# Issuing four early loads from two queues, and loading the branch's integer one step earlier, in a fused windowed-attention and gated-conv kernel

## The chip, the cores and the metric

The kernel runs on one core of one Trainium2 chip. The metric is the device time of one execution in microseconds (us), as the median of several runs. Before the change it is 231.44 us (three runs, 230.78 to 232.59).

The core's engines named below are TensorE (PE), VectorE (DVE), ScalarE (ACT), GpSimd (POOL) and SyncE (SP). SP computes nothing here: it issues DMA transfers. ACT can issue them as well.

## The reference

Two stages over q, k, v of shape (8 batches, 8 heads, 576 positions, 64), in f32:

```python
scores = q @ k.transpose(0, 1, 3, 2) / sqrt(64)
scores = where(abs(pos_i - pos_j) <= 32, scores, -1e9)      # sliding window
attn   = exp(scores - max); attn = attn / (sum(attn) + 1e-9)
x      = (attn @ v).transpose(0, 2, 1, 3).reshape(8, 576, 512)

h    = maximum(x @ w_in, 0)                                  # 512 -> 1024
conv = sum over k of conv_w[k] * h shifted by k - 1          # 3 taps along the sequence
out  = (h * sigmoid(conv)) @ w_out                           # 1024 -> 512
```

The output has the shape (8, 576, 512), f32.

## The kernel before

The work is cut into named operations. An operation is a small piece: a load, a cast, a group of matmuls, a copy out of PSUM. `build` lists them with their dependencies, and the string `PLAN` gives the order in which they are written into the program, with the engine of each copy (`/A` is ACT, `/D` is DVE) and the PSUM banks (`@01`). Each operation is pinned behind what stands before it on its engine (`do`, which calls `keep_in_program_order`), so on each engine the order of PLAN is the order of execution. A few helper instructions are not pinned: the load of the convolution's weights `cw24` (line 399), GpSimd's masks, and `values_load` (line 774).

The operations of the beginning are these:

- `LQK0.yz` loads half z of the positions of k (y = 1) or q (y = 0) of batch 0 into a staging buffer `st` (line 449). It is issued as two transfers, one for each half of the heads (e = 0, 1), each 128 rows of 2,304 bytes, 288 KB. Six staging buffers are used in a ring; a later load into a buffer waits for the cast that reads it.
- `CQK0.yz` casts that buffer to bf16 (line 382 on DVE). It needs both halves.
- `TR0.yz` transposes it on PE (line 393), and `EV0.yz0` and `EV0.yz1` copy the result out of PSUM (line 380 on ACT, line 382 on DVE).
- `MK` builds the four masks and small identity matrices on DVE (lines 421 to 428). The block `start()` (lines 397 to 416) is written ahead of the first word of PLAN that isn't a load: memsets on DVE, a warming activation on ACT (line 398, which brings the load of ACT's function table with it), the issue of `cw24` on ACT, and GpSimd's identity and masks.
- `SC` are the score matmuls, `EX` the exponentials on ACT, `MA` the mask products on DVE, `AV` the products with v, and `F512` filler matmuls on zeros.

In PLAN before, three loads stand ahead of `MK`, and the fourth, LQK0.00, behind it. All eight transfers are issued by SP (`self.dq` is `nc.sync`). The casts follow in the order CQK0.11, CQK0.01, CQK0.10, CQK0.00, all on DVE.

From about 36 us to the end PE works through three streams mixed by PLAN: attention of later batches, the hidden layer (`PH`, relu `RE` on ACT), and the convolution and gate (`CO`, `TA` on ACT, `GA` on DVE) with the output product (`YY`, copy `YC`, store `YS`).

At the end stands a branch. The attention skips the subtraction of the maximum; `OK`, `OM` and `OF` test whether all sums were in range and leave an integer `bad`. `values_load` (line 774) loads it into a register on every engine, and `tc.If(bad > 0)` (line 775) goes to `redo`, a slow version of the whole kernel, if it isn't zero. With the inputs here it is zero: every engine branches past the code of `redo` to the closing barrier (line 802). In the program before, `values_load` is written behind everything else. The last words of PLAN are the output product in the parts YY11.1, YY11.0, YY11.2b and YY11.2a, whose copies are YC11.1 on DVE and YC11.0, YC11.2b and YC11.2a on ACT, each with a store of its own on SP (line 741).

Of the kernel before, what the change touches and what calls it, by code (L numbers as in the profile page):

```python
# [14 lines left out]
B, H, S, D, DM, DF = 8, 8, 576, 64, 512, 1024  # L15
KC, MB, RP, PAD = DM // 128, DF // 128, S // 64, 32
# [56 lines left out]
def build(k, ud=UD):  # L73
# [136 lines left out]

    add("MK", {"DVE": 2.4}, lambda e: k.consts(), w=["mk"])
    load_qk(0, (0,))
    load_qk(0, (1,))
    p = Slot()
    add("CW", {"PE": 0.3}, lambda e: k.conv_w(p), r=[("qkT", 0, y, z, 0) for y in range(2) for z in range(2)], w=["cw"],
# [5 lines left out]
    for u, tls in units():  # L221
        while done_b <= min(B - 1, (2 * u + tls[-1]) // 9):
            for parts in ((0,), (1,)) if done_b < HB else ((0, 1),):
                load_qk(done_b, parts)
            load_v(done_b)
            if done_b == 1:
                weights_out()
            done_b += 1
        attend(u, tls)
        while done_c < NCH and (u > 3 * done_c + 3 - (done_c % 3 == 2) or u == NU - 1) and tls[-1] == 1:  # L230
            ffn(done_c)
            done_c += 1
# [8 lines left out]


PLAN = """
LQK0.11 LQK0.01 LQK0.10 MK LQK0.00 CQK0.11/D LV0.1 TR0.11@01 CQK0.01/D EV0.111/A TR0.01@23 LQK1.00 EV0.110/A
EV0.011/D LQK1.10 CQK0.10/D EV0.010/D TR0.10@30 LV0.4 SC4a@21 CQK0.00/D LV0.2 SC3@45 EX4a.1 EV0.101/A EV0.100/D
LV0.0 TR0.00@16 EX4a.0 LWI3 EV0.001/A MA4a EV0.000/A EX3.1 SC1@16 LWI1 CQK1.00/D SC0@32 EX1.1 SC2@50 CV0.1/D EX0.1
TR1.00@67 LV0.3 EX2.1 CW@2 EV1.001/D EX0.0 EX2.0 CQK1.10/D LWI2 EV1.000/A LWI0 DG EX1.0 F512@0 F512@0 TR1.10@57
# [71 lines left out]
GA10.02 RE11.4 PH11.3@2 RE11.7 TA10.10 CO11.0@7345 RE11.3 GA10.10 PH11.5@6 RO11.1 TA11.00 PH11.1@0 RE11.5 TA11.01  # L319
RO11.3 OM@1 YY10.0@2 RO11.2/D RE11.1 TA11.02 OF GA11.00 TA11.03 GA11.02 CO11.1@7061 YC10.0/D YY10.1@4 GA11.01 TA11.11  # L320
TA11.12 GA11.11 TA11.10 GA11.12 TA11.13 GA11.10 YY10.2@0 YC10.1/A GA11.03 GA11.13 YY11.1@1 YC10.2/D YS10 YY11.0@0
YC11.1/D YS11.1 YY11.2b@1 YC11.0/A YY11.2a@5 YS11.0 YC11.2b/A YS11.2b YC11.2a/A YS11.2a
"""


class Kernel:
# [117 lines left out]
    def load_qk(self, b, y, z, s):  # L444
        st = self.st[s].rearrange("p (e x) -> p e x", e=2)
        if b < HB:
            for e in range(2):
                src = self.qk[y][b, 4 * e:4 * e + 4, 288 * z:, :]
                self.do(self.dq.dma_start(st[:, e], bass.AP(src.tensor, src.offset, [[RP * D, 32], [S * D, 4], [1, RP * D]])))
        else:  # L450
            src = self.qk[y][b, 2 * z:, :, :]
            self.do(self.dq.dma_start(st, bass.AP(src.tensor, src.offset, [[RP * D, 128], [4 * S * D, 2], [1, RP * D]])))
# [291 lines left out]
@with_exitstack  # L744
def kernel(
    ctx: ExitStack,
    tc: tile.TileContext,
    q: bass.AP,
    k: bass.AP,
    v: bass.AP,  # L750
    moe_w_in: bass.AP,
    moe_conv_w: bass.AP,
    moe_w_out: bass.AP,
    out: bass.AP,
):
    kn = Kernel(ctx, tc, q, k, v, moe_w_in, moe_conv_w, moe_w_out, out)
    ops = {op.name: op for op in build(kn).ops}
    names = {"A": "ACT", "D": "DVE", "P": "POOL", "S": "SP"}
    started = False
    for word in PLAN.split():  # L760
        word, _, where = word.partition("@")
        name, _, eng = word.partition("/")
        if not started and not name.startswith("L"):
            kn.start()
            started = True
        if name.startswith("F"):
            kn.fill(int(name[1:]), int(where))
            continue
        op = ops.pop(name)
        for slot, at in zip(op.alloc, where):  # L770
            slot.at = int(at)
        op.emit(names[eng] if eng else next(iter(op.cost)))
    assert not ops
    bad = kn.nc.values_load(kn.bad[0:1, 0:1], min_val=0, max_val=1)
    with tc.If(bad > 0, preferred_fallthrough_block=False):
        kn.redo()

# [29 lines left out]
```

## Time and profile before

| | |
|---|---|
| median of the runs | 231.44 us (230.78 to 232.59) |
| the profiled execution | 233.62 us |
| its span, first to last instruction | 231.9 us, 8,874 instructions |
| granted TensorE clock, mean | 0.991 |
| busy: PE, DVE, ACT | 208.9 us (90%), 190.4 us (82%), 180.5 us (78%) |
| moved by DMA | 49.45 MB, 213 GB/s on average |

The profile is one execution. The span counts from the first to the last instruction on the core; the time of an execution has a little around it. L449 is line 449 of the kernel. A name such as `st<-in_q_dram` says what was written from what. "SPq" and "ACTq" are the issuing queues of those engines, "PEld" the weight loads of TensorE. In a timeline a row gives the start in us, the length in us, the engine, the line and the operation; a bracket at the end gives the idle time ahead of it and what ended that. A chain of waits is followed back from the last instruction, at each step to what released it.

### The profile page before, as it was taken

How to read it: one execution, taken by the hardware profiler on the slowest of the kernel's cores; microseconds unless marked ns; L12 is line 12 of the kernel's file. 1: busy time of each engine (PE TensorE's matmuls, PEld its weight loads, DVE VectorE, ACT ScalarE, POOL GpSimd, SP SyncE). 2: the span in 40 equal slices, each digit the busy share in tenths (PEclk: the TensorE clock that was granted, in tenths of full speed). 3: DMA queues.
4: the chain of work that ended last, by engine and by line, in shares of the span. 5: the costliest groups of instructions: out<-in, count | busy, mean ns of one | idle time of the engine just before them, and what ended most of it. 6: DMA issues, size and time to landing. Idle time of an engine off the chain costs nothing.

```text
span 231.9 us, 8874 instructions
## 1 busy us (share of the span) xinstructions
PE 208.9 (90%) x3741; PEld 122.4 (53%) x3741; DVE 190.4 (82%) x459; ACT 180.5 (78%) x393; POOL 1.2 (1%) x8
## 2 busy tenths in 40 slices
PE   0479789999999999999999999999999879999990
PEld 0354467776455655555655555554545445545450
DVE  7668799999899999999988998889998686655820
ACT  2296688878999999789899989999679577559520
POOL 2000000000000000000000000000000000000000
PEclk9999999999999999999999999999999979999999
DMA  5999599698999994988995984998986926524161
GB/s 154 355 280 309 125 266 217 185 256 219 273 261 328 270 352 131 260 248 251 368 176 114 302 267 90 159 300 197 359 107 206 284 53 105 151 60 160 50 227 56
DMA packets 67187, 49.45 MB, mean 213 GB/s; under 512 B 48044, under 2 KB 53444, under 8 KB 67140
## 3 DMA queue, kind: packets, MB, share of 16 engines
q1 hardware_dynamic: 67104, 48.80, 79.6%
q8 instruction: 31, 0.51, 1.0%
q14 instruction: 16, 0.13, 0.2%
q10 hardware_dynamic: 36, 0.01, 0.0%
HBM read 32.52 MB, written 9.44 MB: 181 GB/s over the span
## 4 chain that ended last, share of the span: by engine, by line
PE 54%; DVE 21%; ACT 8%; DMA 7%; issue 4%; SPq 3%; DVEq 0%; ACTq 0%
PE ps L390 50%; DVE xn L634 5%; PE ps L393 4%; DMA st<-in_q_dram 4%; DVE gT L721 4%; DMA vst<-in_v_dram 3%; DVE vo L382 2%; ACT ps L714 2%; DVE attn L614 2%; ACT attn L543 2%; DVE qkb L382 2%; DVE rec L633 2%; ACT hh L681 2%; SPq L460 2%; DVE ve L382 1%
## 5 line engine op out<-in xcount | busy, mean ns | idle before, releaser
L390 PE MATMUL ps<-xT,w_in_sb 128*128 128x385 bf16 (+3 forms) x448 | 73.1, 308 | 1.0 <-DVE w_in_sb L382 0.3
L390 PE MATMUL ps<-w_out_sb,gT 128*128 128x512 bf16 (+1 forms) x296 | 67.4, 374 | 0.2
L681 ACT ACTIVATE hh<-ps 128x385 bf16<-128x385 f32 (+3 forms) x112 | 47.9, 474 | 10.4 <-PE ps L390 10.2
L721 DVE SCALAR_TENSOR_TENSOR gT<-ps,hh 128x384 bf16<-128x384 f32 x96 | 48.6, 549 | 8.3 <-ACT ps L714 7.2
L390 PEld LDWEIGHTS <-w_in_sb 128*128 128x128 bf16 x448 | 39.8, 99 | 24.6 <-issue 4.3
L714 ACT ACTIVATE ps<-ps 128x384 f32<-128x384 f32 x96 | 42.0, 495 | 6.8 <-PE ps L390 6.1
L543 ACT ACTIVATE attn<-ps 128x512 bf16<-128x512 f32 (+1 forms) x76 | 40.5, 612 | 7.0 <-PE ps L390 3.5
L390 PEld LDWEIGHTS <-gT 128*128 128x128 bf16 x296 | 27.2, 98 | 29.1 <-issue 1.3
L634 DVE TENSOR_TENSOR xn<-ps,rec 128x256 bf16<-128x256 f32 (+1 forms) x76 | 32.2, 424 | 2.6
L380 ACT COPY qkT<-ps 128x576 bf16<-128x576 bf16 x42 | 26.4, 669 | 7.1 <-PE ps L393 7.0
L614 DVE TENSOR_TENSOR attn<-attn,masks 128x1024 bf16<-128x1024 bf16 (+1 forms) x38 | 24.5, 658 | 2.6 <-ACT attn L543 2.4
L393 PE MATMUL ps<-ident,qkb 64*128 64x64 bf16 x576 | 14.5, 199 | 9.8 <-DVE qkb L382 9.1
L380 ACT COPY y<-ps 128x512 f32<-128x512 f32 (+1 forms) x27 | 16.3, 608 | 8.5 <-PE ps L390 8.5
L390 PE MATMUL ps<-hh,diag 32*32 32x384 bf16 x1152 | 20.5, 327 | 0.0
L393 PEld LDWEIGHTS <-qkb 64*128 64x128 bf16 x576 | 11.5, 100 | 15.9 <-DVE qkb L382 11.1
L390 PEld LDWEIGHTS <-attn 128*64 128x64 bf16 x576 | 13.1, 113 | 11.0 <-issue 5.1
L382 DVE COPY qkT<-ps 128x576 bf16<-128x576 bf16 x22 | 16.2, 750 | 2.8 <-PE ps L393 2.6
L382 DVE CAST qkb<-st 128x1152 bf16<-128x1152 f32 x22 | 16.6, 753 | 2.3 <-DMA st<-in_q_dram 2.1
L390 PE MATMUL ps<-ve,attn 128*64 128x65 bf16 x320 | 16.1, 200 | 1.4 <-DVE xn L634 1.0
L390 PEld LDWEIGHTS <-diag 32*32 32x32 bf16 x1152 | 11.9, 88 | 8.0 <-issue 4.4
L633 DVE RECIPROCAL rec<-ps 128x4 f32<-128x4 f32 (+1 forms) x76 | 13.2, 174 | 3.0 <-PE ps L390 2.6
L390 PE MATMUL ps<-vo,attn 128*64 128x65 bf16 x256 | 13.4, 199 | 2.4 <-DVE vo L382 2.1
(57 smaller groups left out, 137.0 us busy)
## 6 DMA issues: line engine op xcount, KB each, us to landing
out_dram<-y SPq DMA_DIRECT2D x11, 768.0 KB, 5.5
st<-in_k_dram SPq DMA_DIRECT2D x12, 576.0 KB, 7.1
st<-in_q_dram SPq DMA_DIRECT2D x12, 576.0 KB, 5.4
vst<-in_v_dram SPq DMA_DIRECT2D x24, 256.0 KB, 5.8
vst<-in_v_dram SPq DMA_DIRECT2D x16, 192.0 KB, 5.5
hh<-hh SPq DMA_DIRECT2D x16, 144.8 KB, 2.9
st<-in_k_dram SPq DMA_DIRECT2D x8, 288.0 KB, 4.8
st<-in_q_dram SPq DMA_DIRECT2D x8, 288.0 KB, 4.5
```

Of the source, the lines that this page charges most:

```text
L380: self.do(nc.scalar.copy(out=out, in_=in_))
L382: self.do(nc.vector.tensor_copy(out=out, in_=in_))
L390: self.do(self.nc.tensor.matmul(*a, **kw))
L393: self.do(self.nc.tensor.transpose(out=out, in_=in_, identity=ident))
L460: self.do(self.dq.dma_start(self.vst[s0 - lo:s1 - lo, c], self.v_[b, :, s0:s1, :].rearrange("h p d -> p h d")))
L543: self.do(self.nc.scalar.activation(at[:, lo:hi], self.ps(ps)[:, lo:hi], AF.Exp, bias=0.0, scale=self.scale))
L614: self.do(self.nc.vector.tensor_tensor(out=at, in0=at, in1=m, op=ALU.mult))
L633: self.do(self.nc.vector.reciprocal(rec, po[:, :, 64]))
L634: self.do(self.nc.vector.tensor_tensor(out=self.xn[x][lo:hi, 4 * g:4 * g + 4, :], in0=po[:, :, 0:64], in1=rec[:, :, None].broadcast_to([hi ...
L681: self.do(self.nc.scalar.activation(o, i_, AF.Relu, bias=0.0, scale=0.5))
L714: self.do(self.nc.scalar.activation(z, z, AF.Tanh, bias=0.0, scale=1.0))
L721: self.do(self.nc.vector.scalar_tensor_tensor(out=o, in0=z, scalar=1.0, in1=self.taps(kind, 0, 128, 6 + 2 * j + g if j else g, 1), op0=ALU ...
```

## The change

Three edits.

In PLAN the fourth load moves ahead of `MK`, and so ahead of the block `start()`. In `load_qk` the second half of the heads (e = 1) of each batch 0 load is issued by ACT, the first half still by SP. That holds for the main path alone; `redo` keeps its queue. And the `values_load` of `bad` becomes a word of PLAN, `VL`, which stands behind YY11.2a, the last matmuls, and ahead of the store of YY11.0 and of the copies and stores of YY11.2b and YY11.2a.

```diff
 PLAN = """
-LQK0.11 LQK0.01 LQK0.10 MK LQK0.00 CQK0.11/D LV0.1 TR0.11@01 ...
+LQK0.11 LQK0.01 LQK0.10 LQK0.00 MK CQK0.11/D LV0.1 TR0.11@01 ...
...
-YC11.1/D YS11.1 YY11.2b@1 YC11.0/A YY11.2a@5 YS11.0 YC11.2b/A YS11.2b YC11.2a/A YS11.2a
+YC11.1/D YS11.1 YY11.2b@1 YC11.0/A YY11.2a@5 VL YS11.0 YC11.2b/A YS11.2b YC11.2a/A YS11.2a
 """
...
         if b < HB:
             for e in range(2):
                 src = self.qk[y][b, 4 * e:4 * e + 4, 288 * z:, :]
-                self.do(self.dq.dma_start(st[:, e], bass.AP(...)))
+                dq = self.nc.scalar if b == 0 and e and not self.general else self.dq
+                self.do(dq.dma_start(st[:, e], bass.AP(...)))
...
+        if name == "VL":
+            bad = kn.nc.values_load(kn.bad[0:1, 0:1], min_val=0, max_val=1)
+            continue
         op = ops.pop(name)
...
     assert not ops
-    bad = kn.nc.values_load(kn.bad[0:1, 0:1], min_val=0, max_val=1)
     with tc.If(bad > 0, preferred_fallthrough_block=False):
         kn.redo()
```

More of the change, by code (lines that the diff above doesn't have):

```diff
@@ L243 @@
 PLAN = """
-LQK0.11 LQK0.01 LQK0.10 MK LQK0.00 CQK0.11/D LV0.1 TR0.11@01 CQK0.01/D EV0.111/A TR0.01@23 LQK1.00 EV0.110/A
+LQK0.11 LQK0.01 LQK0.10 LQK0.00 MK CQK0.11/D LV0.1 TR0.11@01 CQK0.01/D EV0.111/A TR0.01@23 LQK1.00 EV0.110/A
 EV0.011/D LQK1.10 CQK0.10/D EV0.010/D TR0.10@30 LV0.4 SC4a@21 CQK0.00/D LV0.2 SC3@45 EX4a.1 EV0.101/A EV0.100/D
@@ L448, in load_qk @@
                 src = self.qk[y][b, 4 * e:4 * e + 4, 288 * z:, :]
-                self.do(self.dq.dma_start(st[:, e], bass.AP(src.tensor, src.offset, [[RP * D, 32], [S * D, 4], [1, RP * D]])))
+                dq = self.nc.scalar if b == 0 and e and not self.general else self.dq
+                self.do(dq.dma_start(st[:, e], bass.AP(src.tensor, src.offset, [[RP * D, 32], [S * D, 4], [1, RP * D]])))
         else:
```

## The prediction

> **What bounds the kernel now.** I read the page first, then the chain of waits in order of time, then the timeline of the first 12 us and of the last 12 us, where the two edits lie.
>
> ```profile
> span 231.9 us, 8874 instructions
> ...
> PEclk9999999999999999999999999999999979999999
> ...
> PE 54%; DVE 21%; ACT 8%; DMA 7%; issue 4%; SPq 3%; DVEq 0%; ACTq 0%
> ```
>
> The chain that ended last runs over PE for 54% of the span and over VectorE for 21%: in the long middle the engines are full and neither edit touches them. Over transfers it runs for only 7%. The profiled execution took 233.62 us, 1.72 more than its span; the median of the runs is 231.44. One slice (185 to 191 us) had a granted clock of 0.7, and both edits lie outside it, so I take a saving found in the span off the median as it is.
>
> The front, from the chain of waits (start, length, what):
>
> ```profile
> 2.85 4.51 DMA st<-in_q_dram
> ...
> 7.46 0.77 DVE qkb L382
> ...
> 8.98 0.24 DVE qkT L382
> 9.21 0.44 issue
> 9.65 0.76 DVE qkb L382
> ...
> 18.12 6.03 PE ps L390 x31
> ...
> 54.65 0.61 DVE w_out_sb L382
> ...
> 55.27 5.28 DMA st<-in_q_dram
> ```
>
> The first transfer on it is the second half of the second load (LQK0.01, q), issued at 2.85 and landed at 2.85 + 4.51 = 7.36. Behind that stand the cast at 7.46, the transposes, the copy at 8.98, the next cast at 9.65, and so on. The timeline of the same stretch:
>
> ```profile
> 0.81 1.35 SPq L449 DMA_DIRECT2D st<-in_k_dram  x2
> 0.81 0.60 ACTq L399 DMA_DIRECT2D cw<-in_moe_conv_w_dram  x1
> ...
> 1.45 1.28 ACT L398 ACT_TABLE_LOAD   x1 [1.45 <-PEq L791]
> ...
> 2.20 1.25 SPq L449 DMA_DIRECT2D st<-in_q_dram  x2
> ...
> 4.85 0.70 DVE L428 COPY id<-ident 32x32 bf16<-32x32 bf16 x4
> 5.58 0.76 DVE L382 CAST qkb<-st 128x1152 bf16<-128x1152 f32 x1
> ...
> 7.10 1.18 ACT L380 COPY qkT<-ps 128x576 bf16<-128x576 bf16 x2 [4.16 <-PE ps L393]
> 7.46 0.76 DVE L382 CAST qkb<-st 128x1152 bf16<-128x1152 f32 x1 [1.11 <-DMA st<-in_q_dram]
> ...
> 10.46 0.66 PE L393 MATMUL ps<-ident,qkb 64*128 64x64 bf16 x18 [1.52 <-DVE qkb L382]
> ...
> 11.98 1.89 SPq L460 DMA_DIRECT2D vst<-in_v_dram  x1
> ```
>
> The first cast (CQK0.11, 5.58) waits for no transfer: VectorE is busy with the constants until 4.85 + 0.70 = 5.55. The second waits 1.11 us for the transfer. So a faster front is worth at most 1.11 us, and whatever makes the first load land earlier is worth nothing.
>
> **The change, part by part: the loads.** Eight issues leave SP, four of them go to ACT. Two issues take 1.25 to 1.35 us on SP, so about 0.6 each. Now the half issued third at 2.20 and the half issued fourth at 2.85 are both issued second on their queue, at 0.81 + 0.65 = 1.45: 0.75 and 1.4 us earlier. How much of that reaches the landing depends on how busy the transfer engines are. The table by stage gives, in its last three columns, granted clock, DMA share and GB/s:
>
> ```profile
> 2.00:3.00 1.00, 0.00 (x0) 0.00 (x0) 0.78 (x8) 0.93 (x2) 0.32 (x2) 1.00 0.64 106
> 3.00:4.00 1.00, 0.00 (x0) 0.00 (x0) 1.00 (x9) 0.00 (x0) 0.16 (x1) 1.00 1.00 387
> 4.00:5.00 1.00, 0.00 (x0) 0.00 (x0) 0.92 (x6) 0.00 (x0) 0.00 (x0) 1.00 0.87 219
> 5.00:6.00 1.00, 0.00 (x0) 0.00 (x0) 0.93 (x5) 0.00 (x0) 0.00 (x0) 1.00 0.84 263
> 6.00:7.00 1.00, 0.60 (x18) 0.50 (x18) 0.34 (x1) 0.00 (x0) 0.00 (x0) 1.00 1.04 399
> ```
>
> From 3 to 4 and from 6 to 7 they run full, at 387 and 399 GB/s. Between them is a hole, 219 and 263, just where q is first read: it loses (390 - 219 + 390 - 263) / 390 = 0.76 us. The start, 2 to 3 us, loses (390 - 106) / 390 = 0.73 more. A second queue can fill part of both, because two streams are then outstanding instead of one, but it can't pass 390 to 400. The first two loads are 4 x 288 KB = 1,180 thousand bytes. By the rows, 106 + 387 + 219 + 263 = 975 were through at 6.0 and all 1,180 at 6.5; the last engine landed at 7.36, 0.85 later. With the hole filled, the 1,074 that are left at 3.0 take 2.75 us, to 5.75; with the same lag the landing is 6.6, and the cast, 0.1 behind it, starts 0.75 us earlier. With the start filled too, VectorE is the limit (5.58 + 0.76 = 6.34) and the gain is the whole 1.11; with neither it is 0. I take 0.6, four fifths of the hole, since the first q packets of both halves now wait side by side. A loss on the front is the third rival.
>
> [...] No stage of this trace has two large streams at once. [...]
>
> What is late next is the third load: the cast at 9.65 follows the copy at 8.98 directly on VectorE, and its data has to be there at 9.65 - 0.6 = 9.05. It is 590 thousand bytes behind the second, 1.5 us at 390 GB/s, so 8.1 to 8.65: not late. From there the chain is engine work that starts when the step before it ends; the 6.03 us from 18.12 on are PE work in a fixed order, and the later transfer on the chain (55.27) begins where VectorE's cast of 54.65 ends. So the 0.6 stays to the end. SP runs past its issues sooner; the next load into a used buffer waits for the second cast, which moves with it.
>
> On ACT the four issues stand ahead of the table load and of the issue of cw: 0.81 + 4 x 0.65 + 0.60 + 1.28 + 0.20 (the warming activation) = 5.5, and its first copy is due at 7.10. That copy hangs on the first cast, which doesn't move, so 1.6 us of cover hide the move; without the cover ACT would be late by what goes over. Placing LQK0.00 ahead of MK and of the start-up block changes nothing on SP, where the four loads already stand back to back; on VectorE the constants keep their place.
>
> **The word VL.** ACT's last copies, from the timeline:
>
> ```profile
> 224.79 0.37 ACT L380 COPY y<-ps 128x256 f32<-128x256 f32 x1 [0.29 <-PE ps L390]
> 225.66 0.37 ACT L380 COPY y<-ps 128x256 f32<-128x256 f32 x1 [0.50 <-PE ps L390]
> ```
>
> The rows of lines 774 (load) and 775 (branch) (count, ns min/median/max, first and last start), and the last store with its time to landing:
>
> ```profile
> L774 PEldq TENSOR_LOAD <-bad x1: 767/767/767, 223.3 to 223.3; - x1
> L774 ACTq TENSOR_LOAD <-bad x1: 693/693/693, 225.7 to 225.7; - x1
> ...
> L775 PEldq COMPARE_BRANCH  x2: 95/2094/4093, 224.2 to 225.8; - x2
> L775 ACTq COMPARE_BRANCH  x2: 38/44/49, 226.4 to 226.6; - x2
> ...
> out_dram<-y SPq DMA_DIRECT2D x1, 128.0 KB, 3.6
> ```
>
> On PE the load already stands behind the last matmul's issue (223.3), so PE's order doesn't change: its second branch starts at 225.8, takes 4.09 us and ends at 229.9. The last store, issued when the copy of 225.66 ends (226.04) and landed 3.6 later, ends at 229.6. These two set the barrier that opens at 230.3 (row below), and VL moves neither. On ACT the load moves from behind the last copy to ahead of the last two: 0.69 us on an engine that is idle 0.29 and 0.50 before them. The copy of part 2b (224.79) and its store may be late by up to 0.69 - 0.29 = 0.40; the last copy isn't (224.79 + 0.40 + 0.37 = 225.56, due 225.66). ACT's second branch comes up to 0.5 earlier, at 226.1. By itself worth 0 for the barrier.
>
> **Four instructions more on ACT.** Behind the barrier (line 802, window from 230.25 on) one row stands out; below it are the code queues of the page:
>
> ```profile
> L802 ACTq EVENT_SEMAPHORE  x2: 17/17/17, 230.3 to 231.8; - x2
> ...
> L802 POOLq DRAIN  x2: 34/64/93, 230.3 to 230.7; - x2
> L802 SPq DRAIN  x1: 7/7/7, 230.4 to 230.4; - x1
> ...
> L802 PEldq DRAIN  x1: 8/8/8, 230.5 to 230.5; - x1
> ...
> L802 ACTq DRAIN  x1: 135/135/135, 231.5 to 231.5; - x1
> ...
> q8 instruction: 31, 0.51, 1.0%
> q14 instruction: 16, 0.13, 0.2%
> ```
>
> SP and PE drain 0.1 to 0.2 us after 230.3, ACT only at 231.5, with nothing to wait for, and all engines end at 231.8. Code arrives by transfer, 16 pieces of 8 KB on q14 and 31 of 16 KB on q8. PE's 2 x 3,741 instructions in 31 pieces are about 240 each, so the smaller pieces hold about 120. I read ACT's late drain as the first instruction of a new piece, reached too soon after the branch. Four DMA issues on ACT push its end four places further, so that the branch lands inside the new piece and nothing is left to wait for. Then POOL's drain at 230.7 is the next, and the end is 231.6 - 230.7 = 0.9 us earlier. The ends: 0 (the delay has another cause) and 0.95; with the cause right but the border still among ACT's last instructions, the earlier branch alone could give 0.5. I take 0.9. [...]
>
> The sum: 0.6 + 0.9 = 1.5 us; 231.9 becomes 230.4 in the span, and 231.44 becomes 229.9.
>
> **The rivals.** First, the front gives nothing: the engines ran at share 1.00 and 1.04 on both sides of the hole, and if the hole belongs to the first reading of q and not to a lone queue, two queues share the same wait. Against it: the shares of 0.64, 0.87 and 0.84 are room. It gives 231.44 - 0.9 = 230.5. [...]
>
> Second, the end gives nothing: ACT's late drain isn't a matter of place, or another engine, SP with four instructions fewer for one, meets a border in its last instructions. About 4 in 120 places do that, which speaks against the latter. 231.44 - 0.6 = 230.8.
>
> Third, slower: ACT's issues back up. The row at 11.98 shows an issue that took 1.89 us where the queue was full. ACT has until 7.10, so it decides from (7.10 - 0.81 - 2.08) / 4 = 1.05 us an issue. At 1.89 ACT is free at 0.81 + 7.56 + 2.08 = 10.45, its two copies end at 11.63, and the transposes of 10.46, which need the bank that the second copy frees, are 1.2 us late. Without the gain at the end that is 232.6, with it 231.7. Against it: at 1 to 3 us both queues are empty.
>
> Fourth, the scheduler undoes the moves (neither edit reaches the program's order): 231.4.
>
> **How the numbers follow.** Both gains 0.52 (229.9; own range 229.1 to 230.7, from a front of 0.2 to 1.1 and some 0.3 for the runs' median); the end alone 0.17 (230.5); the front alone 0.19 (230.8); slower through ACT 0.07 (231.7 to 232.6); nothing 0.05 (231.4). From 229.1 to 231.3 the range leaves out 2 in 10: the slower case, nothing, and the best of the first. A measurement of this kernel can tell about 1% from no change, 2.3 us: faster means under 229.1, which needs the full 1.11 and 0.95 and a lucky draw, 0.14; slower means over 233.8, 0.04; the rest is within 1%.
>
> **What would show it.** In the changed profile: L449 on both queues by 1.5 us; the second cast starting at 6.6 to 7.2 with less than 1.11 us of wait; the hole at 4 to 6 shallower; ACT's first copy still at 7.1; the chain from the copy at 8.98 on earlier by the same amount; PE's branch still 4.1 us; ACT's last drain within 0.3 us of the others. The prediction is wrong if the second load lands at 7.3 or later, if ACT's drain is still 1 us behind, if ACT's first copy is late, or if the front's gain is eaten by a new wait before 30 us.

## The result, and the profile after

The changed kernel took 228.02 us in the median of five runs (227.81 to 229.58), beside 231.44 us for the kernel before in the same measurement. The ratio is 0.986, 95% interval 0.983 to 0.990. The prediction was 229.9 us with a range of 229.1 to 231.3, so the time fell below the range. Measured twice more beside the kernel before, the same kernel gave ratios of 0.990 (0.985 to 0.995) and 0.989 (0.986 to 0.993). All its 23 runs together have a median of 228.79 us. Medians here are over all runs and ratios over the fast ones; the profiled execution of the kernel before, at 233.62 us, is one of the slow ones (over 1.5% above the fastest). The kernel before stood between 231.22 and 231.59 in the five groups of runs that hold a comparison. So the change is worth 2.7 us rather than the 1.5 us forecast, and about 0.8 us of the first reading was the scatter of five runs.

The profiled execution of the changed kernel took 229.58 us with a span of 227.9 us. Its head, and the line of the granted clock:

```profile
span 227.9 us, 8845 instructions
...
PEclk9999999999999999999999999999999999999998
...
PE 44%; DVE 24%; DMA 11%; ACT 9%; issue 5%; SPq 4%; DVEq 0%; ACTq 0%
```

The slice with a clock of 0.7 is not in every profile with the old loads: that of `vl_only` (below) shows none. So neither it nor the fall of TensorE's share of the chain of waits from 54 to 44% (47% in `vl_only`) is put down to the change. The timeline of its first 12 us, to be laid beside the one of before (in each row start, length, engine and line; a bracket names what the engine waited for):

```profile
0.81 0.72 SPq L450 DMA_DIRECT2D st<-in_k_dram  x1
0.81 0.65 ACTq L450 DMA_DIRECT2D st<-in_k_dram  x1
...
1.49 0.62 ACTq L450 DMA_DIRECT2D st<-in_q_dram  x1
1.59 0.79 SPq L450 DMA_DIRECT2D st<-in_q_dram  x1
...
2.79 0.62 ACTq L450 DMA_DIRECT2D st<-in_q_dram  x1
...
4.93 0.59 ACTq L399 DMA_DIRECT2D cw<-in_moe_conv_w_dram  x1
5.58 0.76 DVE L382 CAST qkb<-st 128x1152 bf16<-128x1152 f32 x1
...
7.10 1.18 ACT L380 COPY qkT<-ps 128x576 bf16<-128x576 bf16 x2 [2.16 <-PE ps L393]
8.31 0.76 DVE L382 CAST qkb<-st 128x1152 bf16<-128x1152 f32 x1 [1.97 <-DMA st<-in_q_dram]
```

The issues are where the prediction put them: both halves of the second load are under way by 1.59 us, ACT needs 0.62 to 0.65 us for one issue, and its first copy is still at 7.10. The table by stage shows the hole filled (the last three columns are granted clock, DMA share and GB/s; before it was 219 and 263 from 4 to 6 us):

```profile
4.00:5.00 1.00, 0.00 (x0) 0.00 (x0) 0.92 (x6) 0.94 (x2) 0.00 (x0) 1.00 1.05 403
5.00:6.00 1.00, 0.00 (x0) 0.00 (x0) 0.93 (x5) 0.00 (x0) 0.00 (x0) 1.00 1.06 360
```

And yet the second cast starts at 8.31, which is 0.85 us **later** than in the profile before (7.46), and it waits 1.97 us where before it waited 1.11. By this pair of profiles the front lost. How the kernel nevertheless became faster by more than forecast is the question of the experiments.

The end looks as forecast. The rows of the closing barrier (line 805 now; count, ns min/median/max, first and last start), and of the branch, line 778:

```profile
L805 ACTq EVENT_SEMAPHORE  x2: 17/17/17, 227.2 to 227.8; - x2
...
L805 POOLq DRAIN  x2: 34/64/93, 227.3 to 227.6; - x2
L805 ACTq DRAIN  x1: 8/8/8, 227.3 to 227.3; - x1
```

```profile
L778 PEldq COMPARE_BRANCH  x2: 95/1974/3853, 221.2 to 222.9; - x2
L778 ACTq COMPARE_BRANCH  x2: 38/46/53, 222.7 to 223.2; - x2
```

ACT's drain, 1.2 us behind the barrier before (231.5 against 230.3), now stands with it at 227.3, and it takes 8 ns where it took 135. The last wave of the barrier follows 0.6 us later (227.2 to 227.8), where it was 1.5 (230.3 to 231.8).

### The profile page after: what moved, and what is told of

Read it like the earlier page. It is cut to its first block, busy times and chain, and to the rows that moved or that the text cites. A ratio compares the mean times of both kernels' runs of the same rounds, so it can differ in the third digit from the quotient of the medians.

```text
span 227.9 us, 8845 instructions
## 1 busy us (share of the span) xinstructions
PE 203.4 (89%) x3711; PEld 121.1 (53%) x3741; DVE 190.1 (83%) x459; ACT 180.2 (79%) x393; POOL 1.2 (1%) x8
## 3 DMA queue, kind: packets, MB, share of 16 engines
HBM read 32.52 MB, written 9.44 MB: 184 GB/s over the span
## 4 chain that ended last, share of the span: by engine, by line
PE 44%; DVE 24%; DMA 11%; ACT 9%; issue 5%; SPq 4%; DVEq 0%; ACTq 0%
PE ps L390 41%; DMA vst<-in_v_dram 6%; DVE gT L722 5%; DVE xn L635 5%; PE ps L393 3%; DMA st<-in_q_dram 3%; ACT hh L682 3%; DVE attn L615 3%; ACT attn L544 2%; DVE vo L382 2%; DVE qkb L382 2%; ACT ps L715 2%; DVE rec L634 2%; DMA hh<-hh 2%; SPq L461 2%
## 5 line engine op out<-in xcount | busy, mean ns | idle before, releaser
L390 PE MATMUL ps<-xT,w_in_sb 128*128 128x385 bf16 (+3 forms) x448 | 72.3, 305 | 1.1 <-DVE w_in_sb L382 0.3
L390 PE MATMUL ps<-w_out_sb,gT 128*128 128x512 bf16 (+1 forms) x269 | 65.0, 373 | 1.8 <-issue 0.5
L390 PEld LDWEIGHTS <-attn 128*64 128x64 bf16 x576 | 12.6, 110 | 10.6 <-issue 5.2
L390 PE MATMUL ps<-ve,attn 128*64 128x65 bf16 x320 | 15.6, 197 | 1.4 <-DVE xn L635 1.0
L390 PEld LDWEIGHTS <-qkT 64*128 64x128 bf16 x576 | 11.1, 99 | 7.5 <-issue 6.0
L390 PE MATMUL ps<-qkT 64*128 64x64 bf16 x576 | 13.5, 196 | 1.7 <-DVE qkb L382 1.3
```

The costliest lines, as they stand in the source:

```text
L390: self.do(self.nc.tensor.matmul(*a, **kw))
```

## The experiments

Two effects had to be separated: the front, with its odd profile, and the end. All times below are medians beside the kernel before on the same chip.

**The change once more, unaltered.** The first question was whether the late cast of 8.31 is what two queues do.

> The changed kernel once more, for a second profile beside its siblings. If the 3.4 us of the first comparison belong to the change: 227.8 to 228.6, a ratio of 0.985 to 0.988. The theory of the code's place expects ACT's last drain within 0.2 us of SP's again. For the front there are two: if the late landing of the second load (8.22 in the first profile) is a matter of one draw, the second cast starts between 6.4 and 7.4 here; if the two queues really delay it, at 8 or later again.

Measured: 229.32 us, ratio 0.990 (0.985 to 0.995), above the 227.8 to 228.6 expected. DVE's casts in its profile's timeline:

```profile
5.58 0.76 DVE L382 CAST qkb<-st 128x1152 bf16<-128x1152 f32 x1
6.54 0.76 DVE L382 CAST qkb<-st 128x1152 bf16<-128x1152 f32 x1 [0.21 <-DMA st<-in_q_dram]
...
8.97 0.76 DVE L382 CAST qkb<-st 128x1152 bf16<-128x1152 f32 x1
```

The same program starts its second cast 1.77 us earlier than in the execution shown first. One execution doesn't tell where a transfer lands: in the one shown first, SP's half of the second load was through in 15 of its 16 parts by 6.62 us, and the last part, which came at 8.22, decided when the cast could start.

**Each part alone.** `split_only` has the new order of loads and the two queues but not VL; `vl_only` has VL (with the lines that read this word, as in the change) but not the loads.

```diff
 # split_only, against the kernel after
-YC11.1/D YS11.1 YY11.2b@1 YC11.0/A YY11.2a@5 VL YS11.0 ...
+YC11.1/D YS11.1 YY11.2b@1 YC11.0/A YY11.2a@5 YS11.0 ...
+    bad = kn.nc.values_load(kn.bad[0:1, 0:1], min_val=0, max_val=1)   # behind the loop again
 # vl_only, against the kernel before
-YC11.1/D YS11.1 YY11.2b@1 YC11.0/A YY11.2a@5 YS11.0 ...
+YC11.1/D YS11.1 YY11.2b@1 YC11.0/A YY11.2a@5 VL YS11.0 ...
```

> Loads on two queues and the order of LQK0.00, without VL. Theory of the code's place: the four issues are enough, ACT's drain within 0.2 us of SP's, and the time is the changed kernel's (228.0 to 228.6). If VL carries part of the gain at the end: drain 0.5 late and about 0.5 slower than the changed kernel. If the loads have nothing to do with the 2 us that aren't at the end: 229.9 to 230.4.

> The kernel before with the word VL alone. Theory of the code's place: ACT's stream has the same length, so the drain is still late, but the branch 0.5 earlier brings it from 1.1 to about 0.6 late: 230.9 (ratio 0.998). Rival (VL is what frees ACT): drain within 0.2, 230.4 (0.9955). No effect at all: 231.4.

Measured: `split_only` 228.71 us, ratio 0.989 (0.983 to 0.995); `vl_only` 231.58 us, ratio 1.000 (0.998 to 1.003). The loads carry the whole change, front and end; VL is worth nothing. This was the third of the cases expected for `vl_only`; the 0.5 us that the first gave to the earlier branch didn't come. In the profile of `vl_only` the branch of ACT is earlier and its drain is as late as ever:

```profile
L804 SPq DRAIN  x3: 7/7/13, 227.6 to 228.0; - x3
...
L804 ACTq DRAIN  x1: 135/135/135, 229.2 to 229.2; - x1
```

So ACT's drain doesn't come late because ACT reaches the barrier late. That also ends the prediction's thought that an earlier branch alone could be worth 0.5.

**The end by itself.** The prediction said that the loads move the end only because four issues lengthen ACT's program. So four, one or two instructions were added to the kernel before at its start, where ACT is idle, and nothing else was changed. They feed nothing.

```diff
         self.do(nc.scalar.activation(self.warm, self.zz[:, 0:1], AF.Exp, bias=0.0, scale=1.0))
+        for _ in range(4):        # act4; 1 in act1, 2 in act2
+            self.do(nc.scalar.activation(self.warm, self.zz[:, 0:1], AF.Exp, bias=0.0, scale=1.0))
```

> The kernel before with four further one-column activations on ACT behind the warming one, at 3 us where ACT is idle: neither edit of the change, only ACT's code four instructions longer. Theory of the code's place: ACT's last drain starts within 0.2 us of SP's (1.1 late before), and the time falls by about 1.0, to 230.4 against 231.4 (ratio 0.995 to 0.997). Rival (the late drain comes from the branch's lateness or something else): drain still 1.1 late, 231.4.

> The kernel before with one more activation on ACT at the start. If ACT's late drain is the first instruction of a new code piece, the piece's border moves one place ahead: now the semaphore instruction between the two drains is the first of the new piece, and the last drain still comes 0.8 to 1.2 us after SP's. If any added instruction at the start frees it: within 0.2.

> The same with two more. The theory of the code's place: the border now lies ahead of the first drain, to which the branch leads, so nothing is left to wait for: last drain within 0.2 us of SP's. If it needed four, or a time and not a place: 0.8 to 1.2 late.

Measured: `act4` 229.82 us, ratio 0.993 (0.990 to 0.996). `act1` and `act2` have one run each, of 230.85 and 230.08 us. The barrier's rows of `act4`, then of `act2`, then of `act1`:

```profile
L804 SPq DRAIN  x3: 7/7/13, 227.8 to 228.2; - x3
L804 ACTq DRAIN  x2: 8/44/80, 227.4 to 228.2; - x2
```

```profile
L804 SPq DRAIN  x3: 7/7/13, 227.5 to 227.8; - x3
L804 ACTq DRAIN  x2: 8/44/81, 227.0 to 227.8; - x2
```

```profile
L804 POOLq DRAIN  x2: 34/64/93, 227.2 to 227.5; - x2
L804 ACTq EVENT_SEMAPHORE  x2: 17/17/17, 228.8 to 229.1; - x2
...
L804 SPq DRAIN  x1: 7/7/7, 228.8 to 228.8; - x1
...
L804 PEldq DRAIN  x1: 8/8/8, 228.8 to 228.8; - x1
L804 ACTq DRAIN  x1: 50/50/50, 228.9 to 228.9; - x1
```

With four and with two more instructions the drain comes with the others. With one more the wait is still there, one instruction earlier: now ACT's part in the barrier itself is late (228.8), and SP, PE and ACT all come 1.3 us after POOL, which was through at 227.5. From the start of the last matmul to the end of the span `act1` takes 6.53 us, the kernel before 6.54, `vl_only` 6.42, `act2` 5.55, `act4` 5.56, `split_only` 5.41 and the changed kernel 5.43. A delay that moves from the drain to the instruction ahead of it when one instruction is added, and disappears with the second, belongs to a place in ACT's program and not to an event that ACT waits for. That it is the border of a piece of code is the author's reading; it fits all of these rows, and the code transfers in the traces agree with it. In every profile an 8 KB piece of code is fetched 0.6 to 0.9 us behind ACT's first drain (at 230.09 behind 229.5 in `before`, at 226.84 behind 226.2 in `after`). In the four profiles with the delay (`before`, `vl_only`, `act1` and `before_f6`, a kernel shown further down) the late instruction starts 1.0 to 1.2 us after this piece has landed (230.57 and 231.54 in `before`, 227.54 and 228.77 in `act1`), and 0.7 to 0.9 us behind it one more piece is fetched (at 232.20 in `before`); the ten other profiles have no such fetch. Which engine a piece belongs to and which instructions it holds is not recorded.

**The two halves against each other.** To size the front, the change and `act4`, which has the same gain at the end, were measured side by side.

> The changed kernel, nothing altered, beside the kernel before with the four added ScalarE instructions alone: the difference between the two is what the front brings to the end. If the 1.1 us by which the two queues bring the first reciprocal forward stays to the end: 1.1 us under act4_again, 228.3 to 229.1. If the wait for the last image's V loads near 185 us takes most of it (TensorE goes on at 184.9 on average in three profiles with two queues, at 185.25 in four with one): 0.2 to 0.4 under, 229.3 to 229.7.

> The kernel before with four one-column activations of ScalarE at its start, which feed nothing; the second measurement of it. The end alone: 1.0 to 1.6 us under the kernel before, 229.8 to 230.4, whatever the front is worth; second cast at 8.0 to 8.4 and TensorE's wait near 185 us ending at 185.0 to 185.7 in its profile. A second cast near 7.5 would mean that the kernel before's profile was no draw apart.

Measured: `after_third` 228.80 us, ratio 0.989 (0.986 to 0.993); `act4_again` 230.22 us, ratio 0.995 (0.993 to 0.998). Over all their runs the kernels with two queues (`split_only` among them, 29 runs) have a median of 228.79, and the two with four added instructions (24 runs) 229.97. So the front is worth 1.2 us at the end, with a standard error of 0.24 worked out from the scatter of these runs. The end is worth 1.1 to 1.6 by the ratios (0.995 and 0.993 of 231.5).

DVE's casts in the timeline of `act4_again`, then of `after_third`:

```profile
5.58 0.76 DVE L382 CAST qkb<-st 128x1152 bf16<-128x1152 f32 x1
7.91 0.76 DVE L382 CAST qkb<-st 128x1152 bf16<-128x1152 f32 x1 [1.57 <-DMA st<-in_q_dram]
```

```profile
6.70 0.76 DVE L382 CAST qkb<-st 128x1152 bf16<-128x1152 f32 x1 [0.36 <-DMA st<-in_q_dram]
...
9.14 0.76 DVE L382 CAST qkb<-st 128x1152 bf16<-128x1152 f32 x1 [0.15 <-DMA st<-in_k_dram]
```

Here are the starts of the second cast in every profile with the loads of one kind or the other, and for those with all their fillers what followed (us; the fillers are the 15 matmuls on zeros ahead of the first product of attention and v, and the first reciprocal is the first work on that product):

| kernel | queues | second cast | fillers start | they take | first reciprocal |
|---|---|---|---|---|---|
| before | 1 | 7.46 | 18.05 | 5.69 | 24.20 |
| before_f6 | 1 | 7.58 | | | |
| act4_again | 1 | 7.91 | 18.57 | 3.41 | 23.36 |
| act2 | 1 | 8.02 | 18.62 | 5.61 | 24.68 |
| act4 | 1 | 8.26 | 18.86 | 5.50 | 24.81 |
| act1 | 1 | 8.38 | 18.98 | 4.95 | 24.38 |
| vl_only | 1 | 8.41 | 19.01 | 5.25 | 24.71 |
| split_only | 2 | 6.53 | 18.00 | 5.11 | 23.56 |
| after_again | 2 | 6.54 | 17.42 | 4.97 | 22.84 |
| warm_after | 2 | 6.55 | | | |
| after_f6 | 2 | 6.70 | | | |
| after_third | 2 | 6.70 | 17.55 | 4.27 | 22.37 |
| after | 2 | 8.31 | 18.92 | 4.63 | 24.00 |

With one queue the median of the second cast is 8.02, with two it is 6.62. The profile before was the earliest draw of its kind and the profile after the latest of its own; the prediction and the first comparison were both read from these. Further on, near 185 us, TensorE waits for the last V loads, and this wait could take the lead back. The first matmul behind that wait, in the timelines of `act4_again` and of `after_third`:

```profile
184.94 0.22 PE L390 MATMUL ps<-vo,attn 128*64 128x65 bf16 x1 [1.16 <-DVE vo L382]
```

```profile
183.57 0.22 PE L390 MATMUL ps<-vo,attn 128*64 128x65 bf16 x1 [1.33 <-DVE vo L382]
```

In this pair the wait takes 0.2 us more with two queues and TensorE is still 1.4 us ahead behind it. Over all profiles of the table with their 15 fillers this matmul comes at 184.6 us on average with two queues (four profiles) and at 185.4 with one (six), 0.8 us apart with a standard error of 0.6, and the wait varies from 0.5 to 2.1 us. So the profiles alone don't show that the whole lead passes this point. The times do: `after_third` and `act4_again` are 1.4 us apart, where a loss here would have left 0.2 to 0.4.

The first reciprocal comes at 24.36 on average with one queue and at 23.19 with two, 1.2 us earlier, as much as the runs' medians differ. It is less than the 1.4 us of the second cast, because behind that stands the third, which needs the third load (k): its median start is 10.38 us with one queue and 9.30 with two, 1.1 us apart. With two queues it waits for its load in three of six profiles, as in `split_only`:

```profile
9.58 0.76 DVE L382 CAST qkb<-st 128x1152 bf16<-128x1152 f32 x1 [0.77 <-DMA st<-in_k_dram]
```

**When ACT's half comes later.** This kernel issues the four loads behind the block of constants, so that ACT issues `cw` first.

```diff
-LQK0.11 LQK0.01 LQK0.10 LQK0.00 MK CQK0.11/D ...
+MK LQK0.11 LQK0.01 LQK0.10 LQK0.00 CQK0.11/D ...
```

> The changed kernel with MK and the start-up block written ahead of the four loads: ACT loads its table first and issues its four halves from 3.0 to 5.6 us, no earlier than SP issued them before; SP's halves keep their early places. If it is the earlier issue that lands the second load early: its last half is issued at 3.6, later than the 2.85 of before, and the second cast starts at 7.4 to 8.4 as with SP alone. If it is two streams side by side: at 6.4 to 6.8. The time: 229.5 to 230.5 in the first case, 228.5 to 229.5 in the second.

Measured: 230.64 us, ratio 0.997 (0.994 to 1.000). The expected times of the issues were wrong: the scheduler put ACT's halves much earlier than the order of words suggests. So neither of the two cases was tried as meant, and the cast fell into neither. ACT's timeline, then DVE's:

```profile
0.81 0.62 ACTq L399 DMA_DIRECT2D cw<-in_moe_conv_w_dram  x1
1.47 0.63 ACTq L450 DMA_DIRECT2D st<-in_k_dram  x1
2.12 1.28 ACT L398 ACT_TABLE_LOAD   x1 [2.12 <-issue]
2.19 0.58 ACTq L450 DMA_DIRECT2D st<-in_q_dram  x1
```

```profile
9.44 0.76 DVE L382 CAST qkb<-st 128x1152 bf16<-128x1152 f32 x1 [3.10 <-DMA st<-in_q_dram]
```

ACT's halves are 0.7 us later than in the change (1.47 and 2.19 against 0.81 and 1.49), and the second cast is later than in any kernel with one queue, although the last half of the second load is issued 0.7 us earlier than there (2.19 against 2.85). The end has its gain (5.58 us from the start of the last matmul), so by its time the front is here about 0.7 us worse than with one queue (230.64 against 229.97, with a standard error of 0.3). The cast needs both halves, so the load is as late as its later half: SP's half, issued at 1.59, landed at 6.7, and ACT's at 9.35, while SP's third load, issued at 2.20, was landing too. Whether that load made ACT's half late is not shown; the profile has no more than the one late landing, so the size of this is a single draw. This kernel also issues `cw` at 0.81 again, where the change issues it at 4.93, and the hole is partly back (353 and 258 GB/s from 4 to 6 us). How much of the front comes from moving `cw` out of the way and how much from the second queue was not separated.

**The fillers.** The table shows that the 15 fillers take from 3.41 to 5.69 us, from one execution to the next, as much as the whole change is worth. The rows of the timelines of `before`, `after` and `act4_again`:

```profile
18.05 5.69 PE L390 MATMUL ps<-zz 128*128 128x512 bf16 x15
```

```profile
18.92 4.63 PE L390 MATMUL ps<-zz 128*128 128x512 bf16 x15
```

```profile
18.57 3.41 PE L390 MATMUL ps<-zz 128*128 128x512 bf16 x15
```

Single fillers start 0.427 us apart up to some moment and 0.216 apart behind it. That moment lay at 22.72 us in the profile before and at 21.45 after, and between 18.6 (or earlier: in `act4_again` all 15 are short) and 23.2 in the others with all fillers and the loads ahead of the constants. The profile's column of the granted clock reads 1.00 throughout, but the trace's records of the clock begin at this very moment (22.70 before, 21.43 after, and within 0.1 us of the change of spacing in every profile where it falls among these fillers), so ahead of it the 1.00 is no reading. So in the profiled pair the fillers gave back what the front lost: they began 0.87 us later and were 1.06 shorter. Do they also swallow a part of every gain at the front? In `after_f6` and `before_f6`, nine of the 15 are taken out.

```diff
-F512@0 F512@0 F512@0 F512@0 F512@0 F512@0 F512@0 F512@0 F512@0 F512@0 F512@0 AV0@57 MA1 ...
+F512@0 F512@0 AV0@57 MA1 ...
```

> The changed kernel with 6 of the 15 fillers ahead of the first attention-times-V product kept and 9 taken out (fillers feed nothing; all results are computed). Theory A (the fillers stand on the path and swallow half of what the front gains): the fillers end at about 19 + 6 x 0.43 = 21.5 us instead of 22.3 to 23.5, and the first product then waits for its mask product or V casts, which the kernel after had ready at 21.3 to 22.7; first reciprocal 22.2 to 23.3 (after: 24.00 and 22.84), and the time is 0.5 to 1 us below that of the kernel after: 227.3 to 228.5. Theory B (the fillers are needed, because the work behind them runs at the spacing of a cold TensorE without them): the reciprocal comes earlier all the same, but matmuls behind it run at half pace for some microseconds more, the lead is gone by 30 us, and the time is that of the kernel after or longer, 228.5 to 230.

> The kernel before with the same 9 fillers out. Theory A: the first product waits for data rather than for fillers, so the first reciprocal stands about 15.5 to 16 us behind the second cast here and in the changed kernel with 6 fillers alike, and the two differ by the whole 1.7 us by which their casts typically differ (8.3 against 6.5), plus 1.1 of the end: 2.5 to 3 us between their times; this kernel itself 0.5 to 1 below the kernel before, 230.4 to 231. Theory B: this kernel is no faster than the one before (231.4 or more), and the two differ by 2 to 3 us as the kernels before and after do.

Measured: `after_f6` 228.03 us, ratio 0.989 (0.984 to 0.993); `before_f6` 231.64 us, ratio 1.001 (0.998 to 1.003). First reciprocals of `before_f6` and of `after_f6`, and the four fillers that follow the second product in each:

```profile
22.75 0.17 DVE L633 RECIPROCAL rec<-ps 128x4 f32<-128x4 f32 x1
```

```profile
21.94 0.18 DVE L634 RECIPROCAL rec<-ps 128x4 f32<-128x4 f32 x1
```

```profile
24.81 1.52 PE L390 MATMUL ps<-zz 128*128 128x512 bf16 x4
```

```profile
24.00 1.89 PE L390 MATMUL ps<-zz 128*128 128x512 bf16 x4
```

Without the nine, the casts of the two profiles differ by 0.88 us (7.58 and 6.70) and their reciprocals by 0.81: in this pair nearly the whole difference arrives. The first product comes earlier, as theory A had it (22.75 against 24.20 before). But `before_f6` isn't faster for it, as theory B had it. `after_f6`, on the other hand, came out in theory A's range, 0.8 us below the 228.79 of the changed kernel; its six runs scatter too much to tell the two apart (the changed kernel's ratio of 0.989 lies within its interval). The slower matmuls that theory B names are in the rows, though not their cause, a TensorE that is cold: the four fillers of 24 to 26 us now take 1.5 to 1.9 us where `act4_again` and `after_third` show 1.04. The trace's clock records go with them: in `before_f6` they begin only at 25.84 us, and in `after_f6` the clock is 1.0 from 19.12 us and 0.5 from 22.54 to 25.95 (0.83 in the mean from 20 to 30 us). The mean granted clock over the runs is lower too, 0.989 and 0.990 against 0.993 for the kernel before and 0.996 to 0.998 for the changed one. So fewer fillers bring the first product forward, and slower matmuls follow. In the kernel before nothing of it is left at the end; for the changed kernel that stays open.

The last kernel went the other way: to the change it adds 20 fillers among the first transposes, so that TensorE is busy before the 15 come.

```diff
-LQK0.11 LQK0.01 LQK0.10 LQK0.00 MK CQK0.11/D LV0.1 TR0.11@01 CQK0.01/D EV0.111/A TR0.01@23 LQK1.00 ...
+LQK0.11 LQK0.01 LQK0.10 LQK0.00 MK CQK0.11/D LV0.1 <12 x F512@7> TR0.11@01 <2 x F512@7> CQK0.01/D EV0.111/A TR0.01@23 <3 x F512@7> LQK1.00 ...
-LV0.0 TR0.00@16 EX4a.0 ...
+LV0.0 TR0.00@16 <3 x F512@7> EX4a.0 ...
```

Here <12 x F512@7> stands for twelve such words.

> The changed kernel with twenty more filler matmuls on zeros: twelve ahead of the first transposes, two and three behind the first two, three behind TR0.00. If the spacing of the fifteen later fillers (0.427 us up to a moment between 20.7 and 23.1, then 0.216) is what holds the first AV back, PE is at the short spacing by 10 us here, all fifteen take 3.3 us, the first reciprocal starts at 21.5 to 22.3 (22.8 to 24.0 so far), and the time is 1 to 1.8 below the changed kernel's: 227.0 to 227.8. If PE falls back to the long spacing in the gaps from 7 to 16 us: no change, 228.5 to 229.3. If the added fillers delay the transposes: slower.

Measured: 229.83 us, ratio 0.991 (0.987 to 0.994), from 227.92 to 232.28. Its 15 fillers took 3.41 us and the first reciprocal came at 22.11, earlier than in any other kernel with all 15, both as the first case expected. Yet it is no faster than the change alone, let alone the 227.0 to 227.8 of that case. Its runs had a mean granted clock of 0.988, but the clock doesn't sort them: the three below 0.980 took 229.8 to 231.6 us, and the longest, 232.28, had 0.990. Why the gain is lost stays open.

## Why the prediction was right or wrong

**The issues and ACT's cover** were right: 0.61 to 0.79 us an issue, ACT's first copy at 7.10 in both. The third rival, issues that back up on ACT, needed over 1.05 us each. That a full queue made the issue at 11.98 last 1.89 us is not shown: the row gives its length alone.

**"So a faster front is worth at most 1.11 us"** is the step that failed first. The 1.11 is the wait of one execution, and it was the shortest wait of all seven profiles with one queue; the median cast at 8.02 leaves 8.02 - 6.34 = 1.68 us. The working then took four fifths of a hole for 0.6. What the two queues bring is 1.4 us at the second cast (8.02 to 6.62), so close to all that there is: the five profiles with two queues other than the first start it within 0.2 us of 6.55. In the times, the term of 0.6 measured 1.2. The forecast of "6.6 to 7.2" for the cast was met by two of six profiles, 6.70 each, three stood at 6.53 to 6.55, just earlier, and the profile after, at 8.31, missed it; by the prediction's own test, "lands at 7.3 or later", that profile would have told against it, and wrongly.

**The first rival.** That the front brings nothing is refuted by 228.79 against 229.97. By the medians the gain is about what the earlier issue saves: the last half of the second load leaves at 1.59 us instead of 2.85, 1.3 us earlier, and the cast behind it starts 1.4 us earlier. A front of nothing, 230.5, gave no weight to this, although the prediction's own working has the two halves issued 0.75 and 1.4 us earlier. Nor do two queues share the same wait in the hole: the stage from 4 to 6 us moves 403 and 360 GB/s with both queues where one moved 219 and 263 (412 and 394 in `after_third`, 288 and 244 in `act4`); 403 and 412 are a little more than the "390 to 400" that the prediction took for the most. From 3 to 4 us one queue moved 387 and two moved 330. But the profile with 403 and 360 is the one whose second load landed late, so a filled hole is not yet an early landing. Whether the earlier issue or the filled hole made the gain was not separated.

**"So the 0.6 stays to the end"** was right in its outcome and wrong in its reason. "The 6.03 us from 18.12 on are PE work in a fixed order" counted them as fixed in length, and they aren't: 15 of those matmuls took 3.41 to 5.69 us. Where they end early enough, something else is last. In the profile after the chain of waits doesn't run over them at all:

```profile
1.59 6.63 DMA st<-in_q_dram
...
8.31 0.77 DVE qkb L382
...
12.84 8.17 DMA vst<-in_v_dram
21.04 0.63 ACT ve L380
...
22.00 0.69 DVE attn L615
...
24.00 0.19 DVE rec L634
```

There it goes from the second cast through SP's queue, where reloads wait for that cast's buffer, to a V load issued at 12.84 and landed at 21.01. Here both ways start at the second cast. They don't in every profile: in `split_only`, `after_again` and `warm_after` the chain starts at the third load, issued at 2.41 to 2.43 and landed at 8.9 to 9.5. So "not late", said of that load, failed as well; it took some 0.3 of the 1.4 us. The 1.2 us at the first reciprocal and the 1.2 in the times agree.

**The 0.9 from the end** was right, and the second rival, no gain there, is refuted. Of its cause the runs show that the delay is a matter of place on ACT, with one, two and four instructions; that the place is the border of a piece of code agrees with the fetches, and no run shows it beyond that. By the profiles it is worth 0.9 to 1.1 us from the last matmul to the end, by the times 1.1 to 1.6. The barrier itself, from its opening to the end of the span, went from 1.60 us (230.29 to 231.89) to 0.65 (227.21 to 227.85), so the step by which POOL's drain leaves a gain of 0.9 came true; what the times show beyond it does not come from the barrier. VL was worth 0, as forecast. PE's second branch, which the prediction put at 4.1 us again, took 3.85 in the profile after (4.09 before, 3.65 to 3.99 in `vl_only`, `act1`, `act2` and `act4`); what it spends this time on is in no row.

**The sum.** Forecast 0.6 + 0.9 = 1.5. Measured 1.2 + 1.5 = 2.7, where 1.5 is the four-instruction kernels' 229.97 under 231.46. Of the missing 1.2 us the front's size is half. The other half is the end, and of that some 0.4 to 0.6 us has no row: the tail is only 0.9 to 1.1 shorter. Whether the granted clock has a part in it is not shown: its mean was 0.9955 in `act4`'s runs and 0.993 in those of the kernel before, but the mean also counts the end, where no engine computes. There the traces record 0.50 from 230.9 us on in `before`, for 1.0 us, and from 226.2 on in `after`, for 1.6 us, which takes 0.002 and 0.004 off the mean, where the two means differ by 0.0025. Where the rest comes from stays open. The chances were wrong where the sum was: "needs the full 1.11 and 0.95 and a lucky draw" described what then happened on average.

## What to carry to other kernels

A wait for a transfer read from one execution is one draw and no bound (the 1.11 us here was the shortest of seven): take a few profiles, or a few related kernels, before you write "at most". At the start of this kernel, cutting each load over two queues brought the second cast forward by 1.4 us, where its last half was issued 1.3 us earlier; with ACT's half issued only at 2.19 us (`late_act`) the cast came at 9.44, later than with one queue. So look that both halves are issued equally early, and then whether the next load becomes the late one, as in three of six profiles here. And when all engines stand in the closing barrier and one drains a microsecond late with nothing to wait for, add two or four idle instructions to that engine, early, and look again: here one left the end at 6.53 us and two brought it to 5.55.

## What the runs showed of the hardware

- The same 15 matmuls took 3.41 to 5.69 us: TensorE's spacing changes from 0.427 to 0.216 us at a moment that moved by more than 4 us between executions (from 18.6 us or earlier in `act4_again` to 23.2), and it didn't follow the data. The trace's clock records begin within 0.1 us of that moment where it falls among these matmuls. What sets it is not shown: all 15 were short, 3.41 us, in `warm_after` with 20 fillers ahead of them and in `act4_again` without.
- On ACT, one instruction more moved a delay from the last drain (231.5 us, 1.1 behind SP's, in `before`) to the barrier, where SP, PE and ACT came 1.3 us behind POOL (`act1`); the second instruction removed it.
- The cast that waits for the second load started at 6.5 to 6.7 us in five of the six profiles of the table with two queues and at 8.3 in one; with one queue it started at 7.5 to 8.4.
- The kernels whose fillers were changed had a mean granted clock of 0.988 to 0.990, against 0.992 to 0.999 for the others. In three profiles the trace records a clock of 0.5 for 3.41 us in mid-kernel: from 186.54 us in `before`, 186.27 in `before_f6` and 22.54 in `after_f6`.
